# Sorting row tiles on ScalarE instead of GpSimd, and three smaller moves, in a gated FFT and GeGLU backward kernel

## The chip, the cores and the metric

The kernel runs on one core of a Trainium2 chip. A core has TensorE (matmuls, in the profile PE, with its weight loads as PEld), VectorE (DVE), ScalarE (ACT), GpSimd (POOL) and SyncE (SP, which here only issues DMAs). Each engine works through its own instructions in order and waits for the others by semaphores. PSUM is the memory that TensorE writes, SBUF the on-chip memory that all engines read. The metric is device microseconds of one execution; lower is better.

## The reference: what is computed

The forward function mixes two branches of an input x of 2048 rows by 576 columns, with a gate g for each row, and the kernel returns its output and seven gradients:

```python
g = sigmoid((x * gate_w).sum(-1, keepdims=True))
a = irfft2(rfft2(x) * (w_r + 1j * w_i))                 # spectral branch
b = (gelu(B_x @ w_gate) * (B_x @ w_up)) @ w_down        # GeGLU branch, F = 4608; x is passed to it
out = g * a + (1 - g) * b
# returned: out and the gradients of x, w_r, w_i, w_gate, w_up, w_down, gate_w for grad_out
```

In `_fwd_reference` both branches get `A_x`: the call is `_B_ref(x, ...)` with `x = A_x`. x, the weights and the outputs are bfloat16. In the text D is the row length 576, F the hidden width 4608.

## The kernel before

**Layout.** The 2048 rows are 16 row tiles of 128 rows (T = 16, P = 128). `xn` and `dB` hold x and grad_out with rows on the partitions; `xT` and `dOT` hold them transposed, with D on the partitions, in four chunks of 128 and a tail of 64 columns (`titems`, `pair`). The chunks are cut by `eo(c)`: chunk c is every fourth column from c on, so partition p of chunk c stands for column 4p + c. The weights have to follow that order. `load_w` brings `w_gate` and `w_up` with a row pattern "(p r)", and `w_down` by a DMA transpose into `wtmp`, a DMA from there to DRAM (`wscr`) and one back into `wdT`, in three parts behind three steps.

**First phase (up to about 910 us).** F is cut in 18 groups of 256 columns (NG), and the rows in 4 blocks of 4 tiles (NPR); one step (`pr` in the main loop) is one group and one block. A step runs `H_mm`: z = dOT·wdT, then xy = xT·wgu for two pairs of row tiles. z has one PSUM buffer (`pz`), xy two (`ph`). ScalarE copies these out (`H_da`, `H_act`: the square q, xb and hu), VectorE makes gelu, its derivative and the products A and dH (`H_ew1`, `H_ew2`). The sigmoids of a step run on ScalarE between. Behind each `H_mm` stand the weight-gradient matmuls of the group before (`W_units`, L584, L602, L616 with two PSUM buffers `wps`, copied out at L553 and stored from the GpSimd queue). `q` has one buffer in SBUF, `xb`, `hu` and `da` have two.

**FFT units.** The transform is cut into units that are strung through the steps from step 7 on, about three in a step (`want`, `fft_next`). For row tile t of x, and later of grad_out, `u1(t)` multiplies six classes of columns (column modulo 6) with a table and ScalarE copies the result Z out of PSUM (L649, L651); `u2(t)` multiplies Z with the table F (L660), ScalarE copies that out as ve (L666), VectorE combines it into Vt, which SP stores (L688). u1 and u2 use the same PSUM buffer as z. The six classes must lie side by side for u1. `sort_x(k)` puts two row tiles of x in that order with one GpSimd copy (L707); `sort_g(t)` does one tile of grad_out and multiplies it with the gate (L720), from a tile `graw` that `load_g` brings. `early` places these by the index of a unit, several units ahead of their use; the first, `sort_x(0)`, stands in step 4, and the second runs at 27 us because nothing on GpSimd holds it back. `build_F` makes the angles of the table F with five VectorE instructions on 294 f32 elements (L126 to L130) in step 3 of the first group, and their sines run later in `run_late`.

**Second phase.** The three remaining products with F as the contraction run from 912 us on (L1207), the inverse transform between them. The change doesn't touch it.

The order of work is the order in which the program is written, per engine; there is no planner beyond `want` and the weights of the units.

The lines that the prediction uses: L418 and L428 copy transposes out, L435 are the gate's matmuls, L456/L461 z, L465/L472 xy, L484 da, L491 q, L493 xb, L494 hu, L499 to L503 `H_ew1`, L519 to L523 the sigmoids, L528 to L540 `H_ew2`, L609 the stores of dw, L972 and L974 the scaling of dB, L284 a table product (Btab), L1272 a copy of the second phase that writes every sixth element.

Of the kernel before, what the change touches and what calls it, by code (L numbers as in the profile page):

```python
# [9 lines left out]
ACT = mybir.ActivationFunctionType  # L10
ALU = mybir.AluOpType
BF16 = mybir.dt.bfloat16
# [8 lines left out]
P, T = 128, 16  # L21
# [7 lines left out]
FG = 256  # L29
# [8 lines left out]
LO, HI = slice(0, 64), slice(64, 128)  # L38
# [3 lines left out]

def eo(c):

    return slice(c, 512, 4)


class Unit:
# [71 lines left out]
def build_F(nc, tb, unit):  # L120

    V = nc.vector
    step = 2.0 * math.pi / D
    X = unit([6, LQ], F32, name="XF")
    y = unit([6, LQ], F32, name="yF")
    V.tensor_tensor(X[:], tb.dcol[:].unsqueeze(2).to_broadcast([P, 6, LQ]), tb.lrow[:].unsqueeze(1).to_broadcast([P, 6, LQ]), op=ALU.mult)  # L126
    V.tensor_scalar(y[:], X[:], 1.0 / D, MAGIC, op0=ALU.mult, op1=ALU.add)
    V.tensor_scalar(y[:], y[:], -MAGIC, -float(D), op0=ALU.add, op1=ALU.mult)
    V.tensor_tensor(X[:], X[:], y[:], op=ALU.add)
    V.scalar_tensor_tensor(y[:], X[:], -1.0, X[:], op0=ALU.mult, op1=ALU.max)  # L130
    tb.F = unit([6, 2, LQ], name="Ft")

    def sines():
        nc.scalar.activation(tb.F[:, :, 0], y[:], ACT.Sin, bias=tb.halfpi[:], scale=-step)
        nc.scalar.activation(tb.F[:, :, 1], X[:], ACT.Sin, scale=-step * EPS_SCALE)
    tb.late.append(sines)
# [155 lines left out]
def kernel(  # L292
# [4 lines left out]
    nc = tc.nc  # L297
    LD = nc.sync
# [4 lines left out]
    dram = ctx.enter_context(tc.tile_pool(name="dram", bufs=1, space=DRAM))  # L303
    res = ctx.enter_context(tc.tile_pool(name="res", bufs=1))
    unit = Unit(ctx.enter_context(tc.tile_pool(name="unit", bufs=NUNIT, side="right")), "unit")
# [3 lines left out]
    wpool = hstack.enter_context(tc.tile_pool(name="wpool", bufs=2, side="right"))  # L309
# [4 lines left out]
    o4v = out_4[0:512, :].rearrange("(c p) f -> p c f", p=P)  # L314
    o5v = out_5[0:512, :].rearrange("(c p) f -> p c f", p=P)
    scr = [[dram.tile([4, P, FF], BF16, name=f"scr{k}_{m}") for m in range(T // 4)] for k in range(3)]
    wscr = [dram.tile([512, FG], BF16, name=f"wscr{k}") for k in range(2)]
    scr_x = dram.tile([P, T, 2, DF], BF16, name="scr_x")
    scr_g = dram.tile([P, T, 2, DF], BF16, name="scr_g")
    kscr = dram.tile([3, P], F32, name="kscr")  # L320
# [9 lines left out]
    xn = wstack.enter_context(tc.tile_pool(name="pxn", bufs=1)).tile([P, T, D], BF16, name="xn")  # L330
    dB = wstack.enter_context(tc.tile_pool(name="pdB", bufs=1)).tile([P, T, D], BF16, name="dB")

    wts = {}
    wtmp = [None]

    def load_w(g, part, tails=LD):

        fsl = slice(g * FG, (g + 1) * FG)
        if g not in wts:
            wts[g] = (wpool.tile([P, 5, 2 * FG], BF16, tag="wgu", name="wgu"), wpool.tile([P, 5, FG], BF16, tag="wdT", name="wdT"))  # L340
        if part == 0:
            wgu = wts[g][0]
            for w, c0 in ((B_w_gate, 0), (B_w_up, FG)):
                cols = slice(c0, c0 + FG)
                LD.dma_start(wgu[:, 0:4, cols], w[0:512, fsl].rearrange("(p r) f -> p r f", r=4))
                for r in (LO, HI):
                    tails.dma_start(wgu[r, 4, cols], w[512:D, fsl])
        elif part == 1:
            wtmp[0] = wpool.tile([P, 4, FG], BF16, tag="wtmp", name="wtmp", bufs=1)
            LD.dma_start_transpose(wts[g][1][:, 4:5, :], B_w_down[fsl, DCH[4][0]:D])  # L350
            LD.dma_start_transpose(wtmp[0][:], B_w_down[fsl, 0:512])
        elif part == 2:
            wdT = wts[g][1]
            LD.dma_start(wdT[LO, 4, :], wdT[HI, 4, :])
            LD.dma_start(wscr[g % 2][:].rearrange("(c p) f -> p c f", p=P), wtmp[0][:])
        else:
            LD.dma_start(wts[g][1][:, 0:4, :], wscr[g % 2][:].rearrange("(p r) f -> p r f", r=4))

    def load_x(t0):
        LD.dma_start(xn[:, t0:t0 + 4, :], x_v[:, t0:t0 + 4, :])  # L360
# [17 lines left out]
    tb = iotas(nc, res, unit)  # L378

    ew = wstack.enter_context(tc.tile_pool(name="ew", bufs=2))  # L380
# [12 lines left out]
    g32 = res.tile([P, T], F32, name="g32")  # L393
# [81 lines left out]

    def ewt(tag, g):
        if tag in ("q", "s", "sg"):
            return unit([4, FG], name=tag) if g == 0 else ew.tile([P, 4, FG], BF16, tag=tag, name=tag, bufs=1)
        return ew.tile([P, 4, FG], BF16, tag=tag, name=tag, bufs=2)

    def H_da(g, m, z):
# [210 lines left out]
    xq, gq, graw = {}, {}, {}  # L692

    def noslot(f):
        f.noslot = True
        return f

    def classes(dst, k):
        q = unit([2, 6, 96], name="xq")
        for j in range(2):  # L700
            dst[2 * k + j] = q[:, j]
        return q

    def sort_x(k):
        def f():
            q = classes(xq, k)
            nc.gpsimd.tensor_copy(q[:], xn[:, 2 * k:2 * k + 2, :].rearrange("p t (q r) -> p t r q", r=6))  # L707
        return noslot(f)

    def load_g(k):  # L710
        def f():
            graw[k] = unit([2, D], name="graw")
            LD.dma_start(graw[k][:], do_v[:, 2 * k:2 * k + 2, :])
        return noslot(f)

    def sort_g(t):
        def f():
            if t % 2 == 0:
                classes(gq, t // 2)
            nc.gpsimd.tensor_scalar(gq[t], graw[t // 2][:, t % 2].rearrange("p (q r) -> p r q", r=6), g32[:, t:t + 1], None, op0=ALU.mult)  # L720
        return noslot(f)

    def turned():
        tp_ = pftile(BF16)
# [154 lines left out]
    for c in range(6):  # L879
        w = gwr[0:1, eo(c)] if c < 4 else gwr[0:1, 512:D]  # L880
        r = slice(0, P) if c < 4 else (LO, HI)[c - 4]
        nc.tensor.matmul(gps[r, c:c + 1], lhsT=w, rhs=one[:], start=True, stop=True)
    AC(gwT[:, 0:4], gps[:, 0:4])
    for c, r in ((4, LO), (5, HI)):
        AC(gwT[r, c:c + 1], gps[r, c:c + 1])
# [11 lines left out]
            f()  # L897
        parity()

    early = {}  # L900
    for k in range(1, T // 2):
        early.setdefault(max(4 * k - 7, 0), []).append(sort_x(k))
    for k in range(T // 2):
        early.setdefault(2 * T + 4 * k - 11, []).append(load_g(k))
    for t in range(T):
        early.setdefault(2 * T + 2 * t - 6, []).append(sort_g(t))
    fg = []
    for i, u in enumerate(zipped(*fwd_units(xq, scr_x, None)) + zipped(*fwd_units(gq, scr_g, SD2))):
        fg += early.get(i, []) + [u]
    mid = mid_units()  # L910
    fft = fg + [turned] + mid

# [63 lines left out]
    for g in range(NG):  # L976
# [3 lines left out]
        for m in range(NPR):  # L980
            pr = g * NPR + m
            n = want(pr) - done[0]
# [13 lines left out]
            if g == 0:  # L996
# [34 lines left out]
                if m == 0:  # L1031
                    build_R(nc, tb, unit, 4)
                    columns_B(nc, tb, res)
                elif m == 1:
                    next(makeB)
                elif m == 3:
                    build_F(nc, tb, unit)
                if m < NPR - 1:
                    gate(m + 1)
                else:  # L1040
# [6 lines left out]
            else:  # L1047
# [23 lines left out]
                state += [*H_ew1(g, tiles, da), da]  # L1071
                if pr == 4:
                    scale_dB(1, VC)
                    sort_x(0)()
                elif pr == 5:
                    build_R(nc, tb, unit, 8)
                    build_R(nc, tb, unit, 12)
# [28 lines left out]
                    sigs()  # L1106
            carry = []
            if m < 3 and g + 1 < NG:
                for part in ((0, 1), (2,), (3,))[m]:
                    load_w(g + 1, part)  # L1110
            if done[0] == n_slots or (pr >= wgT_from and pr % 2 == 0 and len(wgT_all) < 20):
                load_wgT()
# [344 lines left out]
```

## Time and profile before

| | |
|---|---|
| median of 3 runs | 1371.53 us (1370.0 to 1372.75) |
| the profiled execution: its time | 1371.64 us |
| its span in the profile | 1369.9 us |
| TensorE busy | 99% of the span |
| VectorE, ScalarE, GpSimd busy | 66%, 55%, 22% |
| granted TensorE clock, mean | 1.00 |
| data moved by DMA | 214.25 MB, mean 156 GB/s |

A row of a group names line, engine, operation, tiles (out<-in), shape and number, then the busy time in us and the mean ns of one, then the idle time of the engine before them and what ended it. A row of a timeline begins with the start and length in us. A row of waits says who waited for whom, the us in total, how often and the longest. Matmul ends are modelled; starts are measured.

### The profile page before, as it was taken

Reading aid. Unit: us, or ns where it says so; the run is one execution under the profiler, and the core shown is the slowest. Engines: PE = TensorE matmul, PEld = TensorE weight load, DVE = VectorE, ACT = ScalarE, POOL = GpSimd, SP = SyncE. Lnnn points to the kernel's source line nnn. Section 1 sums busy time; section 2 is a strip of 40 time slices with the busy share of each in tenths; the row PEclk is TensorE's granted clock in tenths of the full one; section 3 lists DMA queues with packets and bytes.
Section 4 is the critical chain, followed back from the end, with each engine's and each line's share of the span. In section 5 each row is a group of like instructions: output and inputs, shape, how many; then the busy total and the mean of one; then the engine's idle time right before and its main releaser. Section 6 shows DMA issues by size and latency. Waiting matters only on the chain.

```text
span 1369.9 us, 27195 instructions
## 1 busy us (share of the span) xinstructions
PE 1358.2 (99%) x10408; PEld 904.5 (66%) x10408; DVE 909.0 (66%) x2348; ACT 754.3 (55%) x1357; POOL 301.1 (22%) x508
## 2 busy tenths in 40 slices
PE   9899999999999999999999999999999999999999
PEld 7556656556556655655655655657888888888887
DVE  6989999999867876786786655526536443545320
ACT  6886777777667767776776666622332322223210
POOL 3012234443214532532441311100000000000000
PEclk9999999999999999999999999999999999999999
DMA  6334455445645644744755647599999777788773
GB/s 227 107 112 123 124 136 149 144 133 142 164 129 136 184 118 135 188 135 123 199 136 144 170 119 189 127 220 235 213 218 199 174 157 166 168 158 172 158 147 75
DMA packets 498553, 214.25 MB, mean 156 GB/s; under 512 B 307347, under 2 KB 488278, under 8 KB 498422
## 3 DMA queue, kind: packets, MB, share of 16 engines
q1 hardware_dynamic: 472084, 177.66, 55.3%
q0 software_dynamic: 14912, 24.24, 6.3%
q10 hardware_dynamic: 11426, 10.61, 3.1%
q8 instruction: 81, 1.33, 0.4%
q14 instruction: 50, 0.41, 0.1%
HBM read 45.49 MB, written 93.56 MB: 102 GB/s over the span
## 4 chain that ended last, share of the span: by engine, by line
PE 89%; DVE 6%; DMA 2%; ACT 2%; issue 1%; SPq 1%; POOL 0%; ACTq 0%; DVEq 0%; POOLq 0%
PE acc L1207 29%; PE xy L472 16%; PE wps L602 15%; PE wps L584 10%; PE z L456 8%; PE wps L616 2%; PE xy L465 2%; DMA wd_all<-in_B_w_down_dram 2%; PE z L461 1%; PE acc L1260 1%; PE pf L646 1%; PE acc L1270 1%; PE pf L848 1%; PE pf L770 1%; PE pf L660 0%
## 5 line engine op out<-in xcount | busy, mean ns | idle before, releaser
L1207 PEld LDWEIGHTS <-pin 128*128 128x128 bf16 x3456 | 334.8, 98 | 83.2 <-DMA out_dram<-dw 0.8
L472 PE MATMUL xy<-wgu,xT 128*128 128x512 bf16 x1152 | 270.7, 380 | 0.0
L602 PE MATMUL wps<-dH,xn 128*128 128x512 bf16 x1152 | 265.7, 379 | 1.9 <-DVE dH L540 1.9
L602 PEld LDWEIGHTS <-xn 128*128 128x128 bf16 x1152 | 111.2, 98 | 126.8 <-issue 2.4
L472 PEld LDWEIGHTS <-xT 128*128 128x128 bf16 x1152 | 105.8, 98 | 131.9 <-issue 24.8
L609 POOL DMA_DIRECT2D out_dram<-dw x134 | 74.4, 558 | 394.1 <-ACT dw L553 376.5
L584 PE MATMUL wps<-dB,A 128*128 128x288 bf16 x1152 | 149.8, 286 | 0.7 <-ACT dwd L553 0.7
L1207 PE MATMUL acc<-wd_all,pin 128*128 128x288 bf16 x1152 | 146.7, 286 | 0.0
L1207 PE MATMUL acc<-wgT,pin 128*128 128x288 bf16 x1152 | 146.6, 286 | 0.0
L1207 PE MATMUL acc<-wuT,pin 128*128 128x288 bf16 x1152 | 146.0, 286 | 0.0
L1272 ACT ACTIVATE yo<-acc 128x288 bf16<-128x288 f32 x64 | 67.4, 1245 | 133.7 <-PE acc L1270 118.5
L456 PE MATMUL z<-wdT,dOT 128*128 128x256 bf16 x1152 | 137.7, 273 | 0.1
L584 PEld LDWEIGHTS <-A 128*128 128x128 bf16 x1152 | 112.0, 98 | 34.2 <-issue 0.9
L484 ACT ACTIVATE da<-z,omg 128x256 bf16<-128x256 f32 x288 | 112.0, 472 | 33.3 <-PE z L461 33.2
L1388 DVE TENSOR_TENSOR b16t<-acc,f32t 128x288 bf16<-128x288 f32 x32 | 14.6, 458 | 171.7 <-PE acc L1207 171.6
L456 PEld LDWEIGHTS <-dOT 128*128 128x128 bf16 x1152 | 112.5, 98 | 21.6 <-DVE dOT L428 0.3
L493 ACT CAST xb<-xy 128x512 bf16<-128x512 f32 x144 | 85.1, 591 | 48.5 <-PE xy L472 48.5
L494 ACT CAST hu<-xy 128x512 bf16<-128x512 f32 x144 | 87.4, 607 | 0.0
L491 ACT ACTIVATE q<-xy 128x512 bf16<-128x512 f32 x144 | 80.3, 601 | 11.5 <-DVE s L536 6.4
L1262 ACT CAST Z<-acc 98x384 bf16<-98x384 f32 x64 | 27.5, 481 | 103.5 <-PE acc L1260 103.5
L530 DVE TENSOR_TENSOR xb<-xb,sg 128x1024 bf16<-128x1024 bf16 x48 | 32.9, 686 | 70.6 <-ACT sg L522 70.6
L553 ACT CAST dw<-wps 128x512 bf16<-128x512 f32 x72 | 42.4, 590 | 62.1 <-PE wps L602 61.8
(514 smaller groups left out, 1873.2 us busy)
## 6 DMA issues: line engine op xcount, KB each, us to landing
scr<-dH SPq DMA_DIRECT2D x144, 256.0 KB, 3.5
scr<-A SPq DMA_DIRECT2D x72, 256.0 KB, 2.6
out_dram<-dw POOLq DMA_DIRECT2D x134, 64.0 KB, 1.9
wd_all<-in_B_w_down_dram SPq DMA_DIRECT2D x3, 1728.0 KB, 10.8
out_dram<-dwd POOLq DMA_DIRECT2D x34, 144.0 KB, 3.2
scr_p<-Vt SPq DMA_DIRECT2D x32, 144.5 KB, 2.5
Vp<-scr_p ACTq DMA_DIRECT2D x32, 144.5 KB, 3.7
wgu<-in_B_w_gate_dram SPq DMA_DIRECT2D x18, 256.0 KB, 4.2
```

What stands on the lines that cost most here:

```text
L456: nc.tensor.matmul(zo(t), lhsT=dOT[:, ci, t, :], rhs=wdT[:, ci, :], start=(t % 4 < 2 and ci == 0), stop=False)
L472: nc.tensor.matmul(xy[k][:, t % 2, :], lhsT=xT[:, ci, t, :], rhs=wgu[:, ci, :], start=False, stop=(ci == 3))
L484: nc.scalar.activation(da[:, t, :], z[:, t % 2, t // 2, :], ACT.Copy, scale=omg32[:, 4 * m + t:4 * m + t + 1])
L491: nc.scalar.activation(q[:, h, :], xy[:, :, 0:FG], ACT.Square)
L493: nc.scalar.copy(xb[:, h, :], xy[:, :, 0:FG])
L494: nc.scalar.copy(hu[:, h, :], xy[:, :, FG:2 * FG])
L553: wcopy[0](out, in_)
L584: nc.tensor.matmul(wps[:, :288], lhsT=tl(0, t)[:, fch * P:(fch + 1) * P], rhs=dB[:, t, h * 288:(h + 1) * 288], start=(t == 0), stop=(t == ...
L602: nc.tensor.matmul(wps[:].rearrange("p a b -> p (a b)"), lhsT=xn[:, t, c * P:(c + 1) * P], rhs=kt[t // 4][1][:, t % 4].rearrange("p k f -> ...
L609: wst[0].dma_start(ov[:, c, fsl], dw[:, k, :])
L1207: nc.tensor.matmul(acc[:, :288], lhsT=src[:, r, :], rhs=w_of(r)[:, h * 288:(h + 1) * 288], start=(first and r == 0), stop=(last and r == F ...
L1272: nc.scalar.activation(yv[:, 3 * b:3 * b + 3], ps[:, 0:288].rearrange("p (r q) -> p r q", r=3), ACT.Copy, scale=(SD2, 1.0)[w])
```

## The change

- **Sort.** The GpSimd functions `sort_x` and `sort_g` go. `sort(dst, t)` sorts one row tile on ScalarE, by a copy (x) or an activation with the gate as scale (grad_out). Tiles 0 to 2 of x are sorted in step 4; every later one directly behind a unit u1 (`sorted_after`, odd indices of the list), tile number (i + 5) // 2 behind unit i, which is four units ahead of its use. `load_g` is placed two units earlier.
- **Natural order of D.** `eo(c)` is the contiguous slice of 128 columns. The weights are loaded with "(r p)", the DMA transpose writes `wdT` itself, and `wtmp`, `wscr` and the third part of `load_w` go.
- **q** has two buffers from group 1 on.
- **build_F** is called before the first copies of the kernel, no longer in step 3.

The instructions of TensorE stay the same in number and order. VectorE's differ only in where build_F stands. ScalarE has 32 more, GpSimd 24 fewer, SP 34 fewer.

```diff
 def eo(c):
-    return slice(c, 512, 4)
+    return slice(c * P, (c + 1) * P)
...
-    wscr = [dram.tile([512, FG], BF16, name=f"wscr{k}") for k in range(2)]
-    wtmp = [None]
...
-                LD.dma_start(wgu[:, 0:4, cols], w[0:512, fsl].rearrange("(p r) f -> p r f", r=4))
+                LD.dma_start(wgu[:, 0:4, cols], w[0:512, fsl].rearrange("(r p) f -> p r f", p=P))
...
         elif part == 1:
-            wtmp[0] = wpool.tile([P, 4, FG], BF16, tag="wtmp", name="wtmp", bufs=1)
             LD.dma_start_transpose(wts[g][1][:, 4:5, :], B_w_down[fsl, DCH[4][0]:D])
-            LD.dma_start_transpose(wtmp[0][:], B_w_down[fsl, 0:512])
-        elif part == 2:
-            wdT = wts[g][1]
-            LD.dma_start(wdT[LO, 4, :], wdT[HI, 4, :])
-            LD.dma_start(wscr[g % 2][:].rearrange("(c p) f -> p c f", p=P), wtmp[0][:])
+            LD.dma_start_transpose(wts[g][1][:, 0:4, :], B_w_down[fsl, 0:512])
         else:
-            LD.dma_start(wts[g][1][:, 0:4, :], wscr[g % 2][:].rearrange("(p r) f -> p r f", r=4))
+            LD.dma_start(wts[g][1][LO, 4, :], wts[g][1][HI, 4, :])
...
-            return unit([4, FG], name=tag) if g == 0 else ew.tile([P, 4, FG], BF16, tag=tag, name=tag, bufs=1)
+            return unit([4, FG], name=tag) if g == 0 else ew.tile([P, 4, FG], BF16, tag=tag, name=tag, bufs=1 + (tag == "q"))
...
-    def sort_x(k):
-        def f():
-            q = classes(xq, k)
-            nc.gpsimd.tensor_copy(q[:], xn[:, 2 * k:2 * k + 2, :].rearrange("p t (q r) -> p t r q", r=6))
-        return noslot(f)
...
-    def sort_g(t):
-        def f():
-            if t % 2 == 0:
-                classes(gq, t // 2)
-            nc.gpsimd.tensor_scalar(gq[t], graw[t // 2][:, t % 2].rearrange("p (q r) -> p r q", r=6), g32[:, t:t + 1], None, op0=ALU.mult)
-        return noslot(f)
+    def sort(dst, t):
+        if t % 2 == 0:
+            classes(dst, t // 2)
+        if dst is xq:
+            nc.scalar.copy(xq[t], xn[:, t, :].rearrange("p (q r) -> p r q", r=6))
+        else:
+            nc.scalar.activation(gq[t], graw[t // 2][:, t % 2].rearrange("p (q r) -> p r q", r=6), ACT.Copy, scale=g32[:, t:t + 1])
...
+    build_F(nc, tb, unit)
     AC(gwT[:, 0:4], gps[:, 0:4])
...
-    early = {}
-    for k in range(1, T // 2):
-        early.setdefault(max(4 * k - 7, 0), []).append(sort_x(k))
-    for k in range(T // 2):
-        early.setdefault(2 * T + 4 * k - 11, []).append(load_g(k))
-    for t in range(T):
-        early.setdefault(2 * T + 2 * t - 6, []).append(sort_g(t))
+    early = {2 * T + 4 * k - 13: load_g(k) for k in range(T // 2)}
+
+    def sorted_after(u, n):
+        def f():
+            u()
+            sort(*n)
+        return f
     fg = []
     for i, u in enumerate(zipped(*fwd_units(xq, scr_x, None)) + zipped(*fwd_units(gq, scr_g, SD2))):
-        fg += early.get(i, []) + [u]
+        if i in early:
+            fg.append(early[i])
+        n = (i + 5) // 2
+        fg.append(sorted_after(u, (xq, n) if n < T else (gq, n - T)) if i % 2 and n < 2 * T else u)
...
-                elif m == 3:
-                    build_F(nc, tb, unit)
...
                 if pr == 4:
                     scale_dB(1, VC)
-                    sort_x(0)()
+                    for t in range(3):
+                        sort(xq, t)
...
-                for part in ((0, 1), (2,), (3,))[m]:
+                for part in ((0, 1), (2,), ())[m]:
                     load_w(g + 1, part)
```

## The prediction

> **What bounds the kernel now.** I read the shares of busy time first, then what TensorE waited for, then the timelines around each of its waits.
>
> ```profile
> PE 1358.2 (99%) x10408; PEld 904.5 (66%) x10408; DVE 909.0 (66%) x2348; ACT 754.3 (55%) x1357; POOL 301.1 (22%) x508
> ```
>
> TensorE is busy for 1358.2 of 1369.9 us, and the granted clock is 1.00 nearly throughout. The change leaves the row of TensorE instructions as it is, so at most the 11.7 us of idle time can be won. 3.4 us of those lie behind 1300 us, in the closing steps, which the change doesn't touch. The rest, by releaser:
>
> ```profile
> PE wps L602 <- DVE dH L540: 1.9, 1, 1.9
> PE pf L411 <- DVE dOT L418: 1.6, 1, 1.6
> PE pf L877 <- POOL ident masks.py:199: 1.4, 1, 1.4
> PE pf L646 <- ACT ve L666: 1.0, 3, 0.5
> PE wps L584 <- ACT dwd L553: 0.7, 1, 0.7
> PE pf L646 <- ACT da L484: 0.5, 1, 0.5
> ```
>
> The columns are total, times, longest, in us. Two waits for VectorE stand out: one ends at 35.8 us, one at 60.8 us. The others are waits for ScalarE, at 89, 94, 104, 118, 259 and 311 us. What makes VectorE late is seen in its timeline:
>
> ```profile
> 27.14 1.77 POOL L707 COPY xq<-xn 128x1152 bf16<-128x1152 bf16 x1
> 27.30 2.17 DVE L528 TENSOR_TENSOR dH<-da,xb 128x1024 bf16<-128x1024 bf16 x1
> ...
> 50.92 0.46 DVE L126 TENSOR_TENSOR XF<-dcol,lrow 128x294 f32<-128x294 f32 x1
> 51.42 0.32 DVE L127 TENSOR_SCALAR yF<-XF 128x294 f32<-128x294 f32 x1
> 51.77 0.32 DVE L128 TENSOR_SCALAR yF<-yF 128x294 f32<-128x294 f32 x1
> 52.12 0.47 DVE L129 TENSOR_TENSOR XF<-XF,yF 128x294 f32<-128x294 f32 x1
> 52.61 0.47 DVE L130 SCALAR_TENSOR_TENSOR yF<-XF 128x294 f32<-128x294 f32 x1
> ```
>
> The product at L528 takes 0.68 us in the median and 2.17 us here, from just after the start of a sort on GpSimd until just after its end: VectorE lost 1.49 us. It has no idle time from there to the copy at L418 for which TensorE waits at 35.8 us. The second block is build_F: from 50.92 to the next instruction at 53.00 it holds VectorE for 2.1 us, ahead of the chain that ends in dH for the 60.8 us wait.
>
> Then the stretch in which the row tiles are sorted (columns: length, then busy us and instructions of PE, PEld, DVE, ACT, POOL, then clock and DMA):
>
> ```profile
> 88.00:326.00 238.00, 235.64 (x1793) 143.88 (x1792) 231.54 (x673) 174.91 (x319) 79.02 (x75) 1.00 0.48 132
> ```
>
> VectorE is 97% busy there, ScalarE 73%; TensorE waits 2.4 us all the same, every time for ScalarE.
>
> **The change part by part.** The sum stands against the profiled execution: 1371.64 us, of which the span is 1369.9; the median shown is 1371.53, 0.1 us lower.
>
> *Sorts leave GpSimd.* 8 copies of 1.76 us and 16 scaled ones of 2.58 us (mean) go: 55.3 us of GpSimd, which bounds nothing. What they did to VectorE matters. At 27 us the 1.49 us come back, and the wait of 1.6 us at 35.8 loses them: **-1.5 us**. Next late there is ScalarE's xT copy (33.09 to 34.13 us), done before TensorE would ask. From 88 to 330 us VectorE instructions that overlap a sort are longer than the median of their own line without one by 27 us together; Btab at 85.43 took 3.09 us under two sorts. VectorE gets that back, but TensorE does not wait for VectorE there, so I cost it at nothing; it shortens VectorE's lag. GpSimd's DMA issues (dw, dwd) stood between the sorts and only get earlier.
>
> *build_F in the head.* VectorE is idle from 0.96 to 5.79 us. The five instructions (2.04 us) need dcol and lrow, ready at 1.74 us, so they end near 3.9 us: free. If GpSimd's iotas (until 4.5 us) blocked them for their length they would still end near 5.8 us; bound 0 to 0.5 us, taken 0 because most of those iotas read nothing. At 51 us, 2.1 us of VectorE go; ScalarE's sigmoid at 54.37, which sat idle 2.9 us for VectorE's L500, moves as well, so dH is 2.1 us earlier and the wait of 1.9 us is covered: **-1.9 us**.
>
> *Second buffer for q.* ScalarE's square waited 6.4 us in 5 places for VectorE's last use of q, the longest 2.5 us at 113.2 us. ScalarE's lag from that one made the wait of 0.7 us at 118; another of 1.1 us at 204.2 lies in the same pattern as the two later waits for ve (259 and 311 us, together 0.5 us). These end: **-0.7** and **-0.5 us**.
>
> *Natural order.* The transposes read 128 adjacent columns instead of every fourth. Their weight loads take 113 ns strided against 98 ns for the tails' contiguous ones, but transposes of both kinds start 56 ns apart: nothing. Over the kernel 17 writes of wtmp to DRAM and 17 reloads into wdT go, with SP's waits for them, and the DMA transpose writes wdT itself two steps earlier; TensorE waits for none of these loads: nothing. The loads of wgu keep their packets (rows of 512 bytes).
>
> *Sorts on ScalarE.* 32 instructions of 128x576, reading at a step of 12 bytes. No row shows ScalarE reading so. The nearest:
>
> ```profile
> L522 ACT ACTIVATE sg<-s 128x1024 bf16<-128x1024 bf16 x48 | 50.9, 1060 | 0.6 <-DVE s L500 0.6
> L972 ACT ACTIVATE dB<-dB,omg 128x576 bf16<-128x576 bf16 x12 | 8.4, 799 | 0.0
> L1272 ACT ACTIVATE yo<-acc 128x288 bf16<-128x288 f32 x64 | 67.4, 1245 | 133.7 <-PE acc L1270 118.5 <-DMA do_t<-in_grad_out_dram 15.2
> ```
>
> Lower end: read as if contiguous. 0.83 ns per element (dwd at 288 elements 402 ns, Z at 768 elements 799 ns) takes the 1024-element row down to 0.69 us for an x row; a g row has the scale from a tile, as L972: 0.80 us. Upper end: L1272 writes at that same step of 12 bytes and pays 1245 where the contiguous 288-element copy pays 402, 2.9 ns an element more; on 576 elements 2.4 (x) and 2.5 us (g). I take 0.69 and 0.80, because L972 is the same engine, source and size and only the writing side is known to be slow.
>
> The Trainium skill (SBUF — State Buffer, section Door 1: The DMA port swizzle, the note on cachelines) says that lines are 16 bytes, that a step of up to 8 bf16 is free, and that a line wants two hits. By its first half a step of 6 is free, and with the per-element price of ScalarE: Activation LUTs (What ACT_TABLE_LOAD costs) a row is an estimated 0.67 or 0.76 us, the sum below the same within 0.2 us. Its second half speaks against the change: four elements on three lines is fewer than two hits. L1272 contradicts the first half for writes, and no row here shows reads.
>
> Where does it lie on the path? In steady state it fills ScalarE's idle time: 1.5 rows a step of 12.5 us, 1.1 us into about 3.4 us idle. Examples: after Z at 221.33 ScalarE idles 1.15 us, after 208.50 it idles 1.17, and where it idled for q (204.2) that wait goes. Three places are tight.
>
> - Three x rows after the second dB scaling (61.0 us): 2.1 us, of which 0.89 us were idle. ScalarE is 1.2 us behind until 74; the hu copy then ends at 72.1 instead of 70.9 us, and TensorE's L465 needs its buffer at 72.16: 0.
> - Units 1 and 2, where there is one buffer:
>
> ```profile
> 92.92 0.83 ACT L649 CAST Z<-pf 96x768 bf16<-96x768 f32 x1
> 93.61 0.62 ACT L553 CAST dw<-wps 128x512 bf16<-128x512 f32 x1
> 94.27 0.65 ACT L666 COPY ve<-pf 128x588 f32<-128x588 f32 x1
> ```
>
>  ve ends at 94.92 and the next z matmul starts in that same PSUM tile at 94.97. The sort goes in behind Z, in front of dw and ve: **+0.6 us**.
> - Next step: Z at 100.70, sort, then ve (103.30 to 103.99), for which L646 already waits until 104.04: **+0.7 us**, and 0.1 us at the following z.
>
> Behind the sort on ScalarE stand copies out of PSUM (dw, ve, xy) for TensorE and the sigmoids for VectorE; VectorE has 27 us back, so a sigmoid 0.7 us late costs nothing. Sums: -1.5 -1.9 -0.7 -0.5 = -4.6; +1.4; **-3.2 us**: 1371.64 - 3.2 = 1368.4, from the median 1368.3.
>
> **The rivals.**
>
> 1. *Strided reads cost as strided writes; ScalarE becomes the bound: slower.* 13 x and 16 g rows from 88 to 326 us would take 13 x 2.4 + 16 x 2.5 = 71 us, and ScalarE has 238 - 175 = 63 idle. That is 8 us over, and some 20 if a fifth of the idle time is lost between in-order waits; less the head's 3.4, 1376 to 1388 us. The three tight places cost 5T - 2 us for a row of T (once 3T exceeds 2.1), against 4.6 us of gains: it turns at T = 1.3 us. For it: L1272. Against: nothing shows a reading engine slowed by the step.
> 2. *Half rate (T 1.0 to 1.4 us), or later ScalarE lag elsewhere: no change.* 5T - 2 gives +3 to +5: 1370 to 1372 us.
> 3. *The tight places have slack* that the trace hides because ScalarE only gets there just in time; only the gains remain: 1367 us, and 1366 if the waits at 89 and 94 us (0.7) go too.
> 4. *ScalarE waits for a slot or a load.* Three g sorts take over a buffer that VectorE read three units (12 us) before; VectorE lagged 8 us (102.2 to 110.5). graw is issued eight units ahead. Only a lag above 12 us would stall ScalarE: +2 us each, up to 1373.
>
> **How the numbers follow.** Forecast 0.53 (1367.2 to 1369.7), rival 3 0.10, rival 2 0.18, rival 1 0.12, rival 4 0.07. The bound between a change and none is 0.2%, 2.7 us: 1368.8 and 1374.3. Of the forecast four fifths lie below 1368.8, with rival 3 that makes 0.52 faster; rivals 2 and 4 and the rest of the forecast make 0.36 same, of which I give 0.04 to slower, for a T near 1.4 us with lag elsewhere; slower 0.12 + 0.04 = 0.16. The range takes in rivals 2, 3 and 4 and the lower edge of rival 1, 1365.5 to 1376, and leaves out about 0.12.
>
> **What would show it.** Right: no TensorE wait at 35.8 and 60.8 us; L528 near 0.68 us everywhere; no ScalarE wait of q for VectorE; the sorts at 0.69 and 0.80 us; new waits for ve of 0.6 to 0.7 us near 92 and 101 us. Wrong: sorts above 1.3 us, ScalarE above 95% busy from 88 to 326 us, waits for ve or da in every group, or build_F ending behind 5.8 us with the wdT copy late.

## The result, and the profile after

The changed kernel takes 1368.23 us (median of 9 runs, 1367.81 to 1368.51) against 1371.53 us (1370.0 to 1372.95, 9 runs): a ratio of 0.9976 with a 95% interval of 0.9966 to 0.9986, so 3.3 us faster by the medians. Predicted were 1368.3 us. The profiled execution took 1368.51 us with a span of 1366.7 us, 3.2 us below the span before. The sum is right; several of its terms are not.

What TensorE waits for in the changed kernel, from the view of waits (total us, times, longest). Lines have moved by about 7: L639 was L646, L404 was L411, L577 was L584.

```profile
PE pf L639 <- ACT ve L659: 1.4, 1, 1.4
...
PE pf L420 <- DMA dB<-in_grad_out_dram: 0.9, 1, 0.9
PE z L449 <- ACT ve L659: 0.6, 1, 0.6
...
PE wps L577 <- ACT dw L546: 0.3, 1, 0.3
PE wps L577 <- ACT dB L964: 0.2, 1, 0.2
PE pf L404 <- DVE dOT L411: 0.2, 1, 0.2
```

The 1.9 us for dH is gone, and of the 1.6 us for dOT 0.2 is left. In their place stand waits for ScalarE: 1.4 and 0.6 us for ve, 0.5 for dw and dB. The 0.9 us for a load of dB in the head differs between kernels whose head is the same: e3 and e9 below have none of it, e8 0.5 us. None of the four kernels with the old order of D has that wait, and six of the ten with the natural order have it (0.2 to 0.9 us), so the order may open the way for it; the shift of TensorE's work behind the head, given below, shows no loss by the order.

The product that a sort on GpSimd had held for 2.17 us, in VectorE's timeline:

```profile
27.58 0.69 DVE L521 TENSOR_TENSOR dH<-da,xb 128x1024 bf16<-128x1024 bf16 x1
```

(That sort was the one of the first pair, `sort_x(0)`, called in step 4 and run at 27 us because nothing on GpSimd stood ahead of it. Where the text above calls the sort at 27 us the second one, it should say the first.) The sorts as groups on ScalarE, busy us and mean ns:

```profile
L709 ACT ACTIVATE xq<-graw,g 128x576 bf16<-128x576 bf16 x16 | 17.3, 1081 | 0.0
L707 ACT COPY xq<-xn 128x576 bf16<-128x576 bf16 x16 | 15.7, 994 | 0.0
```

A sorted x row takes 0.99 us and a g row 1.08 us, where 0.69 and 0.80 were taken. One of the prediction's tight places, where ScalarE has little time left before TensorE needs its result, in ScalarE's timeline:

```profile
90.27 0.85 ACT L642 CAST Z<-pf 96x768 bf16<-96x768 f32 x1
90.96 1.06 ACT L707 COPY xq<-xn 128x576 bf16<-128x576 bf16 x1
91.85 0.65 ACT L546 CAST dw<-wps 128x512 bf16<-128x512 f32 x1
92.32 0.72 ACT L659 COPY ve<-pf 128x588 f32<-128x588 f32 x1
```

The sort stands between Z and ve; the next z matmul waits 0.6 us for that ve. The stretch from 88 to 326 us (columns as before):

```profile
88.00:326.00 238.00, 233.84 (x1781) 144.88 (x1803) 208.33 (x687) 199.03 (x344) 30.45 (x54) 1.00 0.44 125
```

VectorE has gone from 231.5 to 208.3 us, ScalarE from 174.9 to 199.0. (81 matmul records are missing from this trace, so its PE column is low.)

**Where the time went.** TensorE's instructions have the same order in all kernels, so the start of each matmul can be held against that of the same matmul before. The shift is constant over long stretches and moves only at a few places. Each cell of this table is such a step in us, the difference of the median shift behind the place and ahead of it, against the one profiled execution of before; places go by that kernel's time. The experiments' rows are discussed below.

| kernel | head | 35.8 | 60.8 | 66, 69 | 93.8 | 95 | 104, 107 | 118 | 208 | 260, 312 | 947 | end |
|---|---|---|---|---|---|---|---|---|---|---|---|---|
| changed | +0.27 | -1.48 | -1.97 | +0.80 | -0.26 | +0.75 | +1.05 | -0.85 | -0.17 | -0.77 | -0.65 | -3.26 |
| e1 angles | -0.21 | 0 | -1.97 | 0 | -0.14 | 0 | 0 | 0 | -0.16 | 0 | -0.65 | -3.13 |
| e11 angles, order | -0.39 | 0 | -1.97 | 0 | -0.13 | 0 | 0 | 0 | 0 | 0 | -0.65 | -3.16 |
| e2 first sort later | -0.46 | -1.47 | 0 | 0 | +1.70 (89 too) | 0 | 0 | 0 | 0 | 0 | -0.65 | -0.87 |
| e5 order | -0.27 | 0 | +1.70 (clock) | 0 | -0.26 | 0 | 0 | -0.37 | -0.17 | 0 | -0.65 | -0.02 |
| e4 order, q | -0.40 | 0 | 0 | 0 | -0.26 | 0 | 0 | -0.85 | -0.17 | -0.76 | -0.65 | -3.09 |
| e7 sorts | -0.66 | -1.47 | +1.70 (clock) | 0 | -0.26 | +0.77 | +1.07 | -0.85 | -0.17 | -0.77 | -0.65 | -1.30 |
| e10 all but the sorts | +0.38 | 0 | -1.97 | 0 | -0.26 | 0 | 0 | -0.84 | -0.17 | -0.76 | +0.76 | -2.88 |
| e3 changed, one q | -0.78 | -1.46 | -1.98 | +0.84 | -0.26 | +0.75 | +1.08 | -0.85 | -0.17 | -0.77 | -0.65 | -4.24 |
| e6 changed, angles back | 0 | -1.46 | 0 | +0.98 | -0.26 | +0.75 | +1.08 | -0.85 | -0.17 | -0.77 | -0.65 | -1.35 |
| e8 changed, read in order | -0.11 | -1.47 | -1.97 | 0 | -0.26 | +0.43 | +0.56 | -0.85 | -0.17 | -0.77 | -0.65 | -5.25 |
| e9 changed, 3 sorts moved | -0.39 | -1.48 | -1.97 | 0 | -0.26 | +0.06 | +0.19 | -0.85 | -0.17 | -0.77 | -0.65 | -6.29 |
| e12 first pair alone | +0.26 | -1.46 | -1.97 | 0 | -0.26 | 0 | 0 | -0.85 | -0.17 | -0.76 | -0.65 | -5.86 |

Two columns say nothing about the change. The head varies by 1.2 us between the executions, and by 1.05 us between the changed kernel and e3, whose heads are the same. The step at 947 us is there in all kernels but e10, also in pairs that share no part: the profiled execution of before lost 0.65 us there, 0.3 of it in a wait for VectorE that the others do not have. The names of the kernels are those of the experiments below.

### The profile page after: what moved, and what is told of

Read it like the earlier page. It is cut to its first block, busy times and chain, and to the rows that moved or that the text cites. A ratio compares the mean times of both kernels' runs of the same rounds, so it can differ in the third digit from the quotient of the medians.

```text
span 1366.7 us, 27046 instructions
## 1 busy us (share of the span) xinstructions
PE 1348.3 (99%) x10327; PEld 903.6 (66%) x10408; DVE 880.7 (64%) x2348; ACT 782.4 (57%) x1389; POOL 245.8 (18%) x484
## 4 chain that ended last, share of the span: by engine, by line
PE 94%; ACT 3%; issue 1%; DVE 1%; DMA 0%; SPq 0%; DVEq 0%; ACTq 0%
PE acc L1198 31%; PE wps L595 17%; PE xy L465 17%; PE wps L577 10%; PE z L449 9%; PE wps L609 2%; PE xy L458 2%; PE z L454 2%; PE acc L1251 1%; PE pf L639 1%; PE acc L1261 1%; PE pf L653 1%; ACT dB L964 1%; PE pf L836 1%; PE pf L758 1%
## 5 line engine op out<-in xcount | busy, mean ns | idle before, releaser
L465 PE MATMUL xy<-wgu,xT 128*128 128x512 bf16 x1081 | 258.0, 379 | 8.5 <-issue 7.1
L577 PE MATMUL wps<-dB,A 128*128 128x288 bf16 x1152 | 149.8, 286 | 0.5 <-ACT dw L546 0.3
L577 PEld LDWEIGHTS <-A 128*128 128x128 bf16 x1152 | 112.0, 98 | 34.1 <-issue 0.9
```

The source lines that it names most:

```text
L465: nc.tensor.matmul(xy[k][:, t % 2, :], lhsT=xT[:, ci, t, :], rhs=wgu[:, ci, :], start=False, stop=(ci == 3))
L577: nc.tensor.matmul(wps[:, :288], lhsT=tl(0, t)[:, fch * P:(fch + 1) * P], rhs=dB[:, t, h * 288:(h + 1) * 288], start=(t == 0), stop=(t == ...
```

## The experiments

**The angles alone (e1).**

```diff
+    build_F(nc, tb, unit)
     AC(gwT[:, 0:4], gps[:, 0:4])
...
-                elif m == 3:
-                    build_F(nc, tb, unit)
```

> The kernel before with build_F moved to the head alone. Theory (VectorE's time at 51 us): the wait of 1.9 us at 60.8 us goes, nothing is added at the head, and no sorts stand on ScalarE to take any of it back: -1.9 to -2.2 us, 1369.4. The wait of 1.6 us at 35.8 us stays, since the sort at 27 us stays on GpSimd. Rival (the gain at 60.8 us in the changed kernel came from VectorE being rid of the sorts): the wait stays and the time is within 0.3 us of before.

Measured: 1368.51 us (1368.27 to 1369.32), ratio 0.9981 (0.9973 to 0.9990). TensorE's waits:

```profile
PE pf L411 <- DVE dOT L418: 1.6, 1, 1.6
...
PE pf L646 <- ACT ve L666: 1.0, 3, 0.5
PE wps L584 <- ACT dwd L553: 0.7, 1, 0.7
```

The wait for dH is gone, everything else stayed: -1.97 us at that place, as expected. In the head build_F costs nothing; these are three of its five instructions and the copy of wdT behind them, in VectorE's timeline:

```profile
1.77 0.47 DVE L126 TENSOR_TENSOR XF<-dcol,lrow 128x294 f32<-128x294 f32 x1 [0.81 <-POOL dcol L77]
...
2.89 0.89 DVE L128 TENSOR_SCALAR yF<-yF 128x294 f32<-128x294 f32 x1
...
4.31 0.47 DVE L130 SCALAR_TENSOR_TENSOR yF<-XF 128x294 f32<-128x294 f32 x1
5.72 0.75 DVE L418 COPY wdT<-fx 128x512 bf16<-128x512 bf16 x2 [0.94 <-PE fx L411]
```

They end at 4.78 us, 0.94 us ahead of the copy.

**One sort, moved in time (e2).**

```diff
+                if pr == 6:
+                    sort_x(0)()
...
                     scale_dB(1, VC)
-                    sort_x(0)()
```

> The kernel before, with the call of sort_x(0) moved from step 4 to step 6, so that GpSimd runs this one copy behind its first stores of dw, after 65 us, and not at 27 us. Theory (the two engines stop each other): the product at L528 near 27 us takes 0.68 in place of 2.17 us and TensorE's wait of 1.6 us at 35.8 us goes, -1.5 to -1.7 us there; the VectorE instruction that meets the sort at its new place loses up to 1.5 us, of which TensorE sees at most that. The wait of 1.9 us at 60.8 us stays. Rival (L528 waits for its own input, or VectorE is late at 35.8 us from other work): L528 and the wait at 35.8 us stay, time within 0.3 us of before.

Measured: 1370.78 us, ratio 0.9998 (0.9989 to 1.0006). The wait at 35.8 us went (-1.47 us), as the lock theory has it, and L528 took 0.69 us at 26.84. What came back is more than expected of one instruction. Timelines of GpSimd, VectorE and ScalarE:

```profile
74.32 1.73 POOL L707 COPY xq<-xn 128x1152 bf16<-128x1152 bf16 x1
84.62 3.40 POOL L707 COPY xq<-xn 128x1152 bf16<-128x1152 bf16 x2
```

```profile
74.20 2.42 DVE L536 TENSOR_TENSOR sg<-sg,q 128x1024 bf16<-128x1024 bf16 x1
84.14 4.17 DVE L284 TENSOR_TENSOR Btab<-oB,msB 128x256 bf16<-128x256 f32 x1 [0.66 <-ACT oB L281]
```

```profile
76.71 1.09 ACT L491 ACTIVATE q<-xy 128x512 bf16<-128x512 f32 x2 [1.28 <-DVE sg L536]
90.80 1.09 ACT L491 ACTIVATE q<-xy 128x512 bf16<-128x512 f32 x2 [1.23 <-DVE sg L536]
```

At its new place the copy held L536 for 1.73 us (2.42 instead of 0.69). L536 is VectorE's last use of q, and q has one buffer, so ScalarE's next square waited 1.28 us. VectorE did not make the 1.73 us good before it copied dwd out at 83.02 us (83.21 before), so the store of dwd, and with it the next two sorts behind it on GpSimd, came hardly earlier than before (84.62 for 84.80); they held Btab until 88.31 us, and the square of the next step waited 1.23 us. TensorE paid 0.62 us at 89 and 1.08 us at 93.8. This shows the whole path by which a sort on GpSimd reaches TensorE: VectorE held, q not free, ScalarE late, TensorE waiting. The kernel before has a little of it at the same place: its square at 91.01 us stands 0.97 us behind the start of Z, with L536 ending at 90.91, where in e7, with no sorts on GpSimd, it stands 0.69 us behind; that accounts for the step of 0.26 us at 93.8.

**The natural order (e5 and e11).** Both have this edit (its main lines); e11 has build_F in the head as well.

```diff
-    return slice(c, 512, 4)
+    return slice(c * P, (c + 1) * P)
...
-            LD.dma_start_transpose(wtmp[0][:], B_w_down[fsl, 0:512])
+            LD.dma_start_transpose(wts[g][1][:, 0:4, :], B_w_down[fsl, 0:512])
```

> The kernel before with the natural order of D alone (contiguous chunks, weights loaded with the other row pattern, no wtmp and no round trip over DRAM). Theory: 0, within 0.3 us of before, with every wait of TensorE where it was. Rival A: the transposes at the head or the loads become faster by up to 1 us. Rival B: the unpredicted loss of 0.3 to 0.5 us at the head of the changed kernel (a wait for the load of dB at 7.7 us) comes from this part, then +0.3 to +0.5 us, and the same wait for a DMA in the profile.

> The kernel before with build_F in the head and the natural order of D; sorts on GpSimd, one buffer for q. Against the kernel with build_F in the head alone (1368.5). Theory (the order costs and wins nothing; what it shows at 118 us beside the second buffer is the buffer's): within 0.2 us of it, with the waits at 118, 259 and 311 us still there. Rival (the order itself ends part of the wait at 118 us, as the kernel with the order alone, under a halved clock, lost 0.37 us there): -0.4 us at 118 us.

Measured: e5 1371.46 us, ratio 1.0000 (0.9991 to 1.0008); e11 1368.61 us, ratio 0.9980 (0.9971 to 0.9989), against 1368.51 us for e1. Behind the head e11 is e1 step for step, except for 0.16 us at 208. So the order is worth nothing, as costed, and rival B of e5 fell: the head's step is -0.27 us, though 0.2 us of the wait for dB are there. The profile of e5 had a surprise, a halved clock at 60 us, told in the last section; with TensorE 1.70 us later from there the small waits for ScalarE at 93.8, 118 and 208 us shrank. e11 has none of that and keeps the 0.7 us at 118: the order does not touch it.

**The second buffer for q (e4 and e3).** A second q takes 2 KB a partition, as much as the natural order frees with wtmp, so the two were tried together. e4 is e5 with

```diff
-... tag=tag, name=tag, bufs=1)
+... tag=tag, name=tag, bufs=1 + (tag == "q"))
```

and e3 is the changed kernel with that line undone.

> The kernel before with the natural order of D and, in the room that it frees, the second buffer for q; the sorts stay on GpSimd and build_F in step 3. Against the kernel with the natural order alone. Theory of the prediction: ScalarE's waits of q for VectorE (6.4 us, 5 times) go, and with them TensorE's waits at 118 us (0.7) and for ve at 259 and 311 us (0.5): -1.2 us. Rival (VectorE's loss to the sorts is the cause, the buffer only the place where it shows): ScalarE no longer waits for q, but TensorE's waits at 118, 259 and 311 us stay, 0 to -0.3 us.

> The changed kernel with one buffer for q in place of two. The kernel with the sorts alone on ScalarE lost TensorE's waits at 118, 208, 259 and 311 us (0.85, 0.17, 0.39, 0.38 us) with one buffer, and the kernel with the order and the second buffer lost them with the sorts on GpSimd. Theory (either of the two ends them, so they were counted twice): within 0.2 us of the changed kernel, step for step, 1368.2, though ScalarE waits for q here and there. Rival (the prediction's: the second buffer is what ends them): these four waits come back, +1.2 to +1.8 us, 1369.4 to 1370.

Measured: e4 1368.83 us, ratio 0.9987 (0.9978 to 0.9996); e3 1368.01 us, ratio 0.9974 (0.9964 to 0.9984). The group of ScalarE's square, its idle time ahead and what ended it, in e1 (one buffer, sorts on GpSimd), in e4 (two buffers, sorts on GpSimd), and in e3 (one buffer, sorts on ScalarE):

```profile
L491 ACT ACTIVATE q<-xy 128x512 bf16<-128x512 f32 x144 | 80.3, 601 | 11.2 <-DVE s L536 6.3 <-PE xy L472 4.5
```

```profile
L484 ACT ACTIVATE q<-xy 128x512 bf16<-128x512 f32 x144 | 80.3, 602 | 5.0 <-PE xy L465 4.5
```

```profile
L484 ACT ACTIVATE q<-xy 128x512 bf16<-128x512 f32 x144 | 80.2, 602 | 4.0 <-PE xy L465 3.4 <-DVE sg L529 0.2
```

The 6.3 us for VectorE go with the buffer, and they go just as well without it once the sorts are off GpSimd. TensorE's steps at 118, 260 and 312 us are the same in both (-0.85 and -0.77), and so are those at 93.8 and 208 us (-0.26 and -0.17). The one at 208 is q as well: before, the square at 205.31 us waited 1.11 us for it, and ve behind it let TensorE go on at 207.97; in e11 that wait is 1.11 us and the step 0, in e1 0.95 us and -0.16. With the sorts on GpSimd the buffer wins these 2.0 us; in the changed kernel it wins nothing that can be seen. In e4 the prediction's theory held; in e3 it fell, and the theory that either part ends the waits held. The waits need both, VectorE late and one buffer.

**The sorts alone (e7), and all but the sorts (e10).** e7 is before with `sort`, `sorted_after` and the new `early`; e10 is the changed kernel with `sort_x`, `sort_g` and the old `early`.

> The kernel before with the sorts on ScalarE alone (placed as in the changed kernel); D stays in its old order, q has one buffer, build_F stays in step 3. Theory now, with the sorts at 0.99 and 1.08 us: -1.5 us at 35.8 us, +2.2 at the tight places (0.8 for the three rows of step 4, 0.5 near 94, 0.9 at 104 us), and the waits that end with a second buffer of q stay: +0.3 to +0.7 us in the sum, same as before. Theory of the prediction (the tight places cost 1.4 and the waits for q stay): -0.1 us. Rival (VectorE without the sorts is early enough that one buffer of q does): another -1.5 to -2.0 us, 1369.5 or less.

> The changed kernel with the sorts put back on GpSimd (and load_g back in its old place); the natural order, the second buffer for q and build_F in the head stay. Theory (the parts add up, and the sort's move costs 2.2 and wins 1.7 us): the wait of 1.6 us at 35.8 us is back, the waits for ve and dw at 66 to 104 us that the changed kernel has are gone: 0.4 to 0.6 us below the changed kernel, 1367.7. Rival (the sorts on GpSimd cost VectorE 27 us, which shows once nothing else is in the way): 1 to 2 us above the changed kernel, 1369 to 1370.5.

Measured: e7 1371.02 us, ratio 0.9995 (0.9986 to 1.0004), against 1371.84 for before in the same runs; e10 1367.83 us (1366.77 to 1369.01), ratio 0.9968 (0.9957 to 0.9979). TensorE's waits in e7:

```profile
PE wps L602 <- DVE dH L540: 1.9, 1, 1.9
PE pf L646 <- ACT ve L666: 1.4, 1, 1.4
...
PE z L456 <- ACT ve L666: 0.6, 1, 0.6
```

Here the rival of e7 held by its waits: those at 118, 260 and 312 us ended with one buffer. Its time, 1369.5 us or less, did not come out. The profiled execution had the halved clock too, +1.70 us. Without that, and with 0.98 us at 66 and 69 us (e6, where TensorE is not slowed), the sorts alone come to -1.47 - 0.26 + 0.77 + 1.07 - 0.85 - 0.17 - 0.77 + 0.98 = -0.7 us.

In e10 the waits for ve and dw are gone and the wait at 35.8 us is back, as the theory has it. The difference to the changed kernel, over the places that differ, is -1.48 + 0.80 + 0.75 + 1.05 = +1.1 us for the changed kernel. The medians differ by only 0.4 us; in e10's profiled execution, at 1368.88 us, TensorE waits for loads of the second phase, which it does in no other of these profiles:

```profile
PE acc L1199 <- DMA pin<-scr: 1.1, 2, 0.7
```

So, by the steps, taking the sorts off GpSimd costs 1.1 us with the other parts in place; the medians point the same way, but their intervals overlap. Of the whole, the angles win 1.97 us, the waits for q 2.05 and the first sort 1.48; the tight places take 2.60 back.

**What the step of 12 bytes costs (e8).**

```diff
-            nc.scalar.copy(xq[t], xn[:, t, :].rearrange("p (q r) -> p r q", r=6))
+            nc.scalar.copy(xq[t], xn[:, t, :].rearrange("p (r q) -> p r q", r=6))
```

and the same in the activation.

> The changed kernel with the 32 sorts reading their row in order in place of every sixth element, so that the columns of a class are the wrong ones; size, engine and place stay. Theory (the step of the reading costs 0.3 us a row): an x row 0.69 and a g row 0.80 us, and the tight places cost 0.8 less at 66 to 69 us and 0.3 less each at 94 and 104 us: -1.2 to -1.5 us against the changed kernel, 1366.9. Rival (a copy from SBUF of this size takes 0.99 us in any order): rows and time unchanged.

Measured: 1366.49 us (1366.30 to 1366.80), ratio 0.9959 (0.9947 to 0.9972).

```profile
L709 ACT ACTIVATE xq<-graw,g 128x576 bf16<-128x576 bf16 x16 | 12.3, 768 | 0.0
L707 ACT COPY xq<-xn 128x576 bf16<-128x576 bf16 x16 | 10.7, 684 | 0.0
```

Read in order the rows take 0.68 and 0.77 us, the prediction's lower end. The step adds 0.31 us to both, 0.54 ns for each of 576 elements, a fifth of the 2.9 ns that L1272 pays for writing at that step. TensorE's cost at the tight places (the steps from 66 to 107 us without the one at 93.8) falls from 2.60 to 0.99 us.

**Other places for three sorts (e9), and the first pair alone (e12).** e9:

```diff
+                if pr == 8:
+                    sort(xq, 4)
                 for f in inside:
                     f()
+                if pr == 6:
+                    sort(xq, 2)
...
-                    for t in range(3):
+                    for t in range(2):
...
                     sigs()
+                if pr == 7:
+                    sort(xq, 3)
```

with the first sort behind a unit being that of row 5. e12 is e10 with this in step 4:

```diff
-                    sort_x(0)()
+                    q = classes(xq, 0)
+                    for t in range(2):
+                        nc.scalar.copy(q[:, t], xn[:, t, :].rearrange("p (q r) -> p r q", r=6))
```

> The changed kernel with three sorts moved into idle time of ScalarE: row 2 from step 4 into step 6 behind the copy of dwt (1.37 us idle there), row 3 from behind unit 1 to the end of step 7 behind the sigmoid (1.37 us idle), row 4 from behind unit 3 to step 8 behind da (0.69 us idle). Theory (the three tight places are tight because of where the sorts stand): the waits at 66 to 69 us (0.8), 94 us (0.5) and 104 us (0.9) go, -2.0 to -2.2 us, 1366.1. Rival (ScalarE is behind all along from 52 to 104 us, and a sort anywhere there comes out at TensorE): waits for da, Z or ve appear at 88 to 98 us in their place, 0 to -0.8 us.

> The changed kernel with all sorts back on GpSimd but for the first pair of x rows, which ScalarE sorts in step 4 with two copies. Theory (the only thing that taking the sorts off GpSimd wins is VectorE's 1.49 us at 27 us, and the other 30 rows cost ScalarE's tight places more than they win): the wait of 1.6 us at 35.8 us is gone, no wait at 66 to 104 us is new, -1.5 us against the kernel with all sorts on GpSimd, 1366.0, and so within 0.3 us of the kernel with three sorts moved. Rival (two sorts in step 4 are late already, or the sorts on GpSimd show elsewhere once the first is gone): 1366.6 or more, with a wait for dw, dB or VectorE at 62 to 95 us.

Measured: e9 1365.57 us (1365.31 to 1366.94), ratio 0.9956 (0.9943 to 0.9968); e12 1365.60 us (1365.10 to 1365.90), ratio 0.9954 (0.9939 to 0.9969). Two of e9's sorts in ScalarE's timeline, and what followed:

```profile
90.23 0.65 ACT L659 COPY ve<-pf 128x588 f32<-128x588 f32 x1
90.78 1.06 ACT L512 ACTIVATE s<-s 128x1024 bf16<-128x1024 bf16 x1
91.73 0.98 ACT L707 COPY xq<-xn 128x576 bf16<-128x576 bf16 x1
93.21 1.56 ACT L477 ACTIVATE da<-z,omg 128x256 bf16<-128x256 f32 x4 [0.49 <-PE z L454]
94.64 1.02 ACT L707 COPY xq<-xn 128x576 bf16<-128x576 bf16 x1
```

ve now comes straight behind dw, and the sort lies where ScalarE waited for z; 0.49 us of that wait are left. Of 2.60 us at the tight places 0.25 remain. What is left of e12's waits, without those of the head:

```profile
PE pf L639 <- ACT ve L659: 0.5, 1, 0.5
PE pf L639 <- ACT da L477: 0.5, 1, 0.5
PE acc L1192 <- ACT dw L546: 0.4, 1, 0.4
PE pf L404 <- DVE dOT L411: 0.2, 1, 0.2
```

e12 keeps 30 of 32 rows on GpSimd and has all of the gain and no tight place. VectorE still loses time to the sorts from 88 to 326 us (231.91 us busy, as before), and TensorE does not see it with two buffers for q. Against the changed kernel's 1368.23 us, and its end of -3.26 in the table, both are 2.6 to 3.0 us faster; between the two the runs do not tell.

**The angles back in step 3 (e6).** The changed kernel with e1's edit undone.

> The changed kernel with build_F back in step 3. TensorE's wait of 1.9 us at 60.8 us is back: +1.97 us, less the 0.8 us at 66 and 69 us that the three sorts of step 4 cost only because TensorE is early: +1.2 us. Theory on the clock (in two of the five profiles that have this wait the granted clock fell to 0.50 for 3.4 us directly behind it, +1.70 us, and in none of the five without): some of the executions lie another 1.7 us higher, so that the times spread over 1.5 us or more, from about 1369.4 up to 1371 or above, where the changed kernel's spread over 0.7. Rival (the clock falls by chance, with no tie to the wait): the times spread over less than 1 us around 1369.4.

Measured: 1370.38 us (1369.76 to 1370.70), ratio 0.9990 (0.9982 to 0.9999). The time expected, 1369.4 us, was missed. The 1.9 us are back, but the cost at 66 and 69 us did not go: 0.98 us. ScalarE is late with TensorE: its sigmoid of that step is idle for 2.90 us, until VectorE, behind build_F, has made the input (L493 ends at 52.84), and starts at 52.93 instead of 51.05. The scaling of dB and the three sorts start as much later:

```profile
52.93 1.06 ACT L512 ACTIVATE s<-s 128x1024 bf16<-128x1024 bf16 x1 [2.90 <-issue]
59.41 2.81 ACT L707 COPY xq<-xn 128x576 bf16<-128x576 bf16 x3
```

The twelve times spread over 0.94 us and not over 1.5, so the theory on the clock missed the spread. But the mean clock on record is 0.999 in three of the twelve, and these are the three longest (1370.67 to 1370.70 us); it is 1.000 in all nine executions of the changed kernel. So the clock is no accident of the profile; the last section has the count.

## Why the prediction was right, and where it was not

*GpSimd no longer holds VectorE at 27 us, -1.5.* Right: -1.48 here, -1.47 in e2, where only that sort moved. The Trainium skill (SBUF — State Buffer, section Who interferes with whom) says that a VectorE instruction with two inputs in SBUF and a GpSimd instruction that reads SBUF exclude each other for the whole instruction. The traces agree: 2.17 us under a copy of 1.77, 2.42 under one of 1.73, 0.69 without.

*build_F in the head, 0 there and -1.9 at 60.8.* Right: 0 and -1.97. The reason for taking nothing, that most of the iotas on GpSimd read nothing, did not hold: in e1 L127 and L128 took 0.58 and 0.89 us where they take 0.32 in step 3, each beside iotas that ran from 1.76 to 2.68 and from 2.79 to 3.61 us. The angles ended at 4.78 us and not near 3.9; within the idle time of VectorE, so the bound held and the price stayed 0. That ScalarE's sigmoid moves along was right too, and e6 shows it from the other side.

*Natural order, nothing.* Right (e11), though it was not idle: it freed the 2 KB that the second q takes.

*Second buffer for q, -0.7 and -0.5.* The place and the size are about right (-0.85, -0.77), the cause is half. The step that failed is the sentence ahead of it, that TensorE does not wait for VectorE from 88 to 330 us and that the 27 us it gets back are therefore worth nothing. TensorE does not wait for VectorE directly; ScalarE waited for it, for q, and TensorE for ScalarE. So taking the sorts off GpSimd wins the same 1.6 us by itself (e7), and the buffer then wins nothing (e3). The same path gave 0.26 us at 93.8 and 0.17 at 208, which the prediction left out: 2.05 us for its 1.2. Counted once, as the prediction did, the gain belongs to either part; the prediction gave it to one.

*T, the time of one sorted row, 0.69 and 0.80.* The term that was mis-sized: 0.99 and 1.08 us. The choice of the lower end for "only the writing side is known to be slow" was wrong by a third of a microsecond. The Trainium skill's note on cachelines (SBUF — State Buffer, section Door 1: The DMA port swizzle) calls a step of up to 8 bf16 free; e8 and the changed kernel show +0.31 us for 576 elements at a step of 6, so the measurement decides against that half, and its other half, at least two hits a line, points the right way.

*The tight places, +1.4.* They were the right ones, but the first, put at nothing, costs as much as the others: for 0, 0.6, 0.7 and 0.1 the runs showed 0.80, 0.75, 0.87 and 0.18. The first follows from T: three rows of 0.99 us no longer fit, and the copies of dw and dB came late, not the hu copy that was named. With T as predicted (e8) it is 0, and the sum 0.99. The prediction's formula, 5T - 2, gives 2.95 for T = 0.99 and 1.4 for 0.68; measured were 2.60 and 0.99, so its slope held (1.61 us for 0.31) and its constant was 0.4 too high.

*Why the sum still held.* The tight places cost 1.2 us more than predicted, and the path over q won 0.85 us more; 0.65 us at 947 us are a chance of the profiled execution before, and 0.3 us went in the head. The cost and the gain were both put too low, and chance made up the last 0.4 us. That they cancel is luck; the sum is closer than its terms.

*The rivals.* Strided reads as slow as writes: no, 0.31 instead of 1.7 us more. Half rate (T from 1.0 to 1.4, given 1370 to 1372): T was at its edge, and its price of +3 us was nearly right; its time did not come out, because its formula is 0.4 too high and the gains came out larger. No slack hidden: e8 and e9 show the places are real. ScalarE waiting for a slot or a load: not seen.

## What to carry to other kernels

Parts of a change that end the same wait are worth that wait once, so undo each of them in the full version as well as trying it alone; here the headline part cost 1.1 us, by the steps of the traces, once the others were in. Before work moves to another engine to free a locked one, ask which of the locked instructions anybody is late for: once q had two buffers, one sort of 24 mattered, and moving only that one gained 2.6 us more than moving all. And the idle share of an engine says little about where a microsecond fits: ScalarE is busy for 57% of the span, and three sorts moved into its idle time cost 2.35 us less.

## What the runs showed of the hardware

The granted clock fell to 0.50 for about 3.4 us in two profiled executions, both directly behind TensorE's wait of 1.9 us near 60 us. e5, by windows (clock is the column before the last two):

```profile
60.00:61.00 1.00, 0.49 (x2) 0.21 (x2) 0.90 (x3) 0.73 (x2) 0.00 (x0) 0.77 0.03 7
61.00:62.00 1.00, 1.00 (x4) 0.35 (x3) 1.00 (x3) 0.38 (x1) 0.00 (x0) 0.50 0.56 160
62.00:63.00 1.00, 1.00 (x3) 0.30 (x2) 1.00 (x3) 1.00 (x3) 0.00 (x0) 0.50 0.88 219
63.00:64.00 1.00, 1.00 (x4) 0.42 (x3) 1.00 (x4) 1.00 (x4) 0.00 (x0) 0.52 0.72 210
```

Each cost 1.70 us. Six profiles have that wait and two of them the halved clock; eight do not have the wait and none has it there. The mean clock on record for each execution says the same: it is 1.000 in all 67 executions of the changed kernel, e1, e3 and e8 to e12, which lack the wait, and below that (0.998 or 0.999) in 17 of 56 of e2 and e4 to e7, which have it. Three of e4's eleven are below; they took 1370.36 us in the median and the other eight 1368.68, the same 1.7 us. In e6 only 0.3 us lie between, and e2's two took no longer than its others: the mean does not say where in the execution the clock fell, nor how much of the loss waits behind it took back. In these kernels, then, a stall of this kind is in some executions dearer than its length: e1's median gained 2.6 us, its steps at 60.8 to 208 us 2.3.

The Trainium skill (TensorE: Matmul & The Clock Gate, Part 1: The HAM clock gate) says that the clock is halved after an idle window of about 3.4 us, in windows that run freely. The length agrees: in all fourteen traces the stretches between two changes of the clock are whole multiples of 3.413 us, and both spells at 0.50 are one such window long. But the idle time was only 1.9 us at a stretch, and four profiles with the same wait kept a clock of 1.00. In the window of 3.413 us that ended when the clock fell, TensorE was busy for 1.48 us (e5) and 1.44 us (e7). In the four that kept it, the emptiest window around the wait had 1.48 (e2), 1.50 (before), 1.81 (e4) and 2.25 us (e6, where the wait falls into two windows). It fits that the place of the wait in the window decides, but e2 and e5 are too near each other to show it: what decides stays open.
